# Longer load runs and 64 by 64 transposes for Q, K and V in a fused attention and spectral-mix kernel

## The chip, the cores and the metric

The kernel runs on one core of one Trainium2 chip. The metric is the device time of one execution in microseconds, the median of several runs; smaller is better. A core has TensorE (PE, matrix multiplication and transposes, with a row of its own for weight loads, PEld), VectorE (DVE), ScalarE (ACT), GpSimd (POOL), SyncE (SP), and 16 DMA engines that carry all transfers.

## What is computed

Sliding-window causal attention over 8 batches, 8 heads, 576 tokens and 64 values per head, then a Fourier-domain mix of the lowest 64 modes with a complex weight matrix for each mode, and a channel product with a rectifier:

```python
# attention: q, k, v are (8, 8, 576, 64) float32
scores = matmul(q, k.T) / sqrt(64)
mask   = (rel >= 0) & (rel < 64)            # rel = query position - key position
attn   = softmax(where(mask, scores, -1e9))
x      = matmul(attn, v)                    # heads side by side: (8, 576, 512)

# spectral mix: w_r, w_i are (64, 512, 512), w_ch is (512, 512)
X  = rfft(x, axis=1)[:, :64]                # 64 modes
Y  = X @ (w_r + i w_i), mode by mode
u  = x + irfft(Y, n=576)
out = u + relu(u @ w_ch)                    # (8, 576, 512) float32
```

The mode weights are most of the input: 127 matrices of 512 by 512 float32 values are read (the imaginary one of mode 0 isn't needed). Q, K and V are 24 pieces (three for each batch) of 8 x 576 x 64 float32 values, 1.18 MB each as they are read. GpSimd's DMAs turn float32 into bf16 on the way, so half as many bytes are written as are read.

## The kernel before

Q, K and V of a batch come as `[tokens, 64]` per head and are needed as `[64, tokens]`, two heads above each other in the 128 partitions: head group `hh` (heads 4 hh to 4 hh + 3) takes partitions 64 hh to 64 hh + 63. The partition of a loaded tile is a pair of head `g` within its group and run `p` of 18 tokens; the two head groups lie beside each other in a partition:

```python
RUN = S // 32                                # 18 tokens

def raw_tile(which):
    return rawp.tile([128, 2, RUN * D], BF16, name="r" + which)

def load(b, which):
    r = raw_tile(which)
    nc.gpsimd.dma_start(
        out=r, in_=RAW[which][b].rearrange("(x g) (p c) d -> (g p) x (c d)", g=4, c=RUN))
    raws[b, which] = r
```

A transpose then takes one token of each run, for all 128 partitions of one head group, and writes 64 rows by 128 columns of PSUM. Twelve of them (6 tokens, 2 groups) fill a PSUM tile, which one instruction of ScalarE or VectorE puts into its places:

```python
def part(src, dst, c0, on_act):
    def f():
        ps = ps_misc.tile([128, 6, 128], BF16, name="pst", tag="misc")
        for c in range(6):
            for hh in range(2):
                nc.tensor.transpose(out=ps[64 * hh:64 * hh + 64, c, :],        # L226
                                    in_=src[:, hh, (c0 + c) * D:(c0 + c + 1) * D],
                                    identity=ident_bf)
        evac(view(dst, c0, [[S, 4], [RUN, 32], [1, 6]]),                       # L58, L59
             view(ps, 0, [[32, 4], [1, 32], [128, 6]]), on_act)
    return f
# ... cut: vback turns V back into token rows (L243)
return [part(rk, kT, 0, True), part(rk, kT, 6, False), part(rk, kT, 12, True),
        # ... the same three for rv and rq, then vback(0), vback(1), vback(2)
```

These twelve units of a batch are spread among the windows of the batch before it. A window has scores (L299, 64 by 64 tiles of the TensorE array), an exponential on ScalarE (L305), the product with V (L324, mostly 128 rows by 64 columns), and the mask for the next window (L280, 64 by 64; L274 for the first six windows):

```python
scores(w)
weigh(w - 1, 8 * w - 8, cut)
if todo: todo.pop(0)()                       # a unit
mask(w + 1, max(1, 3 - n))
if todo: todo.pop(0)()
weigh(w - 1, cut, 8 * w)
while todo: todo.pop(0)()
```

Whenever a unit has used up a raw tile, POOL issues the load of the batch after next into it, and a load of a weight matrix (L117). After attention the weights stream through a set of buffers; each mode (L592) uses its two matrices and hands their buffers back to POOL, which loads the next ones (L122: two matrices in one DMA). The output stage (L742, L903, L926) follows when the last mode has been used.

```python
for im, w in enumerate((wr, wi) if m else (wr,)):
    for c in range(NC):
        # ... cut
        nc.tensor.matmul(out=psy[r0:r0 + k, :], lhsT=xq(c, m, im, [[NM, k]]), rhs=w[:, c, :], ...)  # L592
    # ... cut
    refill_w(m, im)                          # L117, L122: loads into the buffers that came free
```

Of the kernel before, what the change touches and what calls it, by code (L numbers as in the profile page):

```python
# [11 lines left out]
BF16 = mybir.dt.bfloat16  # L12
# [8 lines left out]
def view(ap, off, dims):  # L21

    return bass.AP(ap.tensor, ap.offset + off, [list(ap.ap[0])] + [list(d) for d in dims])
# [3 lines left out]
def kernel(  # L27
# [10 lines left out]
    nc = tc.nc  # L38
    B, H, S, D = q.shape
# [5 lines left out]
    NT = 5  # L45
    NC = DM // 128
    VW = 66
    RUN = S // 32
    LW = 5
    EW = 13  # L50

# [3 lines left out]
    def evac(o, i, on_act):  # L55

        if on_act:
            return nc.scalar.copy(out=o, in_=i)  # L58
        return nc.vector.tensor_copy(out=o, in_=i)  # L59
# [8 lines left out]
    ident_bf = consts.tile([128, 128], BF16, name="ident_bf")  # L68
# [11 lines left out]
    rawp = p1.enter_context(tc.tile_pool(name="rawp", bufs=2, side="right"))  # L80
# [5 lines left out]
    ps_misc = p1.enter_context(tc.tile_pool(name="ps_misc", bufs=3, space=PSUM))  # L86
# [5 lines left out]
    RAW = {"k": k, "q": q, "v": v}  # L92

    def raw_tile(which):
        return rawp.tile([128, 2, RUN * D], BF16, name="r" + which)

    def load(b, which):
        r = raw_tile(which)
        nc.gpsimd.dma_start(
            out=r, in_=RAW[which][b].rearrange("(x g) (p c) d -> (g p) x (c d)", g=4, c=RUN))  # L100
        raws[b, which] = r


# [23 lines left out]
    warm = acons.tile([128, 512], BF16, name="warm")  # L127
    nc.vector.memset(warm, 0.0)
    load(0, "k")
    load(0, "q")  # L130


# [39 lines left out]

    nc.scalar.activation(out=warm[:, 0:1], in_=ident[:, 0:1], func=ACT_F.Exp)
    load(0, "v")
    nc.vector.tensor_copy(out=ident_r, in_=ident)
    idp.close()
# [6 lines left out]
    for i in range(4):  # L183
        half = i % 2
        pp = slice(64 * (i // 2), 64 * (i // 2) + 64)
# [27 lines left out]
    def transpose_units(b):  # L213

        rk, rq, rv = (raws.pop((b, which)) for which in "kqv")
        qT = qtp.tile([128, 4, S], BF16, name="qT")
        vT = vtp.tile([128, 4, S], BF16, name="vT")
        kT, vt = kTs[b % 2], vts[b % 2]
        qTs[b] = qT

        def part(src, dst, c0, on_act):
            def f():
                ps = ps_misc.tile([128, 6, 128], BF16, name="pst", tag="misc")
                for c in range(6):
                    for hh in range(2):
                        nc.tensor.transpose(out=ps[64 * hh:64 * hh + 64, c, :],  # L226
                                            in_=src[:, hh, (c0 + c) * D:(c0 + c + 1) * D],
                                            identity=ident_bf)
                evac(view(dst, c0, [[S, 4], [RUN, 32], [1, 6]]),
                     view(ps, 0, [[32, 4], [1, 32], [128, 6]]), on_act)  # L230
            return f

        def vback(u):
            def f():
                ps = ps_misc.tile([128, 6, 128], BF16, name="psv", tag="misc")
                for i in range(6):
                    a, j = divmod(6 * u + i, 9)
                    if j == 4:
                        parts = [(0, 64, 2 * a, 512), (64, 64, 2 * a + 1, 0)]
                    else:  # L240
                        parts = [(0, 128, 2 * a + (j > 4), 128 * j - (j > 4) * S)]
                    for r0, n, g, t0 in parts:
                        nc.tensor.transpose(out=ps[r0:r0 + n, i, :],  # L243
                                            in_=vT[:, g, t0:t0 + n], identity=ident_bf)
                evac(view(vt, 6 * u * VW, [[18 * VW, 2], [VW, 6], [1, D]]),
                     view(ps, 0, [[D, 2], [128, 6], [1, D]]), u != 1)
                if u:
                    hs = slice(u - 1, u + 2, 2)
                    nc.vector.tensor_copy(out=vt[64:128, 1, hs, 1:9], in_=vt[64:128, 0, hs, 0:8])
                    nc.vector.tensor_copy(out=vt[0:64, 1, hs], in_=vt[0:64, 0, hs])  # L250
            return f

        return [part(rk, kT, 0, True), part(rk, kT, 6, False), part(rk, kT, 12, True),
                part(rv, vT, 0, False), part(rv, vT, 6, True), part(rv, vT, 12, False),
                part(rq, qT, 0, True), part(rq, qT, 6, False), part(rq, qT, 12, True),
                vback(0), vback(1), vback(2)]

    def head_of(n):
# [5 lines left out]
    for half in range(2):  # L264
        pp = slice(64 * half, 64 * half + 64)
# [119 lines left out]
    def refill(b, j):  # L385

        which = {2: "k", 5: "v", 8: "q"}.get(j)
        if which is None:
            return
        if b + 2 < B:  # L390
            load(b + 2, which)
        elif nw < EARLY:
            early(EARLY)
        if b:
            early(1)
        if b + 2 >= B:
            spare(raw_tile(which))
# [3 lines left out]
    with tc.manual_schedule(engines={mybir.EngineType.PE, mybir.EngineType.Pool}):  # L401
        warm_up(7)
        first = transpose_units(0)
        for i, j in enumerate((0, 1, 2, 6, 7, 8, 3, 4, 5, 9, 10, 11)):
            first[j]()
# [16 lines left out]
        def unit(b, j):  # L422
            if b not in units:
                units[b] = transpose_units(b)
            units[b][j]()
            refill(b, j)
# [175 lines left out]
    with ExitStack() as p2a:  # L602
# [30 lines left out]
        for m in range(L0 * MG):  # L633
            mode(m)
            if m == 1:
                for b in range(1, B, 2):
                    tc.keep_in_program_order(nc.scalar.copy(out=x_sb[64:128, b - 1, NT - 1, :],
                                                            in_=x_sb[64:128, b, NT - 1, :]))
# [181 lines left out]
    with tc.manual_schedule(engines={mybir.EngineType.PE}):  # L820
        for m in range(M0, ME):
            while len(spreads) > 5 * B // 2 * (ME - 1 - m) // (ME - M0):
                b0, h = spreads.pop(0)
# [54 lines left out]
    with tc.manual_schedule(engines={mybir.EngineType.PE, mybir.EngineType.Activation, mybir.EngineType.DVE,  # L878
                                     mybir.EngineType.Pool, mybir.EngineType.SP}):
        nc.vector.tensor_copy(out=view(YT2, R - RL, [[NR, NC], [R, 2], [1, RL]]),  # L880
                              in_=view(psl, 0, [[RL * B, NC], [RL, 2], [1, RL]]))
# [103 lines left out]
```

The softmax here doesn't subtract the row's maximum and nothing guards it: scores larger than these inputs give would overflow.

## Time and profile before

| what | value |
|---|---|
| device time, median of 3 | 426.12 us (426.09 to 426.28) |
| span of the profiled execution | 424.3 us, mean granted TensorE clock 0.927 |
| TensorE busy | 348.0 us (82%) |
| VectorE, ScalarE, GpSimd busy | 184.5, 171.2, 78.9 us |
| bytes written by GpSimd's DMAs | 81.80 MB in 24864 packets |
| memory read in all | 162.53 MB, 405 GB/s over the span |

The page cuts the span into 40 equal slices and gives, for each, the busy share of an engine in tenths. Attention lies in the first third, the weight stage ends near slice 36, and the output stage fills the rest. A matmul's duration in this trace is the time from its start to the end of its last result, and matmuls are pipelined, so what a run of them costs is read from the distance of their starts. In the DMA part, GB/s count what is written; a transfer that turns float32 into bf16 reads twice that. In the list of waits, each line reads: who waited, for whom, us in total, how often, longest.

### The profile page before, as it was taken

The numbers are of one execution on the slowest core, as the hardware profiler recorded it, in microseconds if no ns is written. First come the engines' busy times: TensorE is split into PE (matmuls) and PEld (weight loads), VectorE is DVE, ScalarE is ACT, GpSimd is POOL, SyncE is SP. The second block draws the span as 40 slices with busy tenths as digits, with TensorE's granted clock in tenths as the row PEclk, the third lists the DMA queues.
The fourth block names the chain that finished last, engine by engine and source line by source line (L and its number), as shares of the span: only waits on it lengthen the run. The fifth ranks groups of instructions, "written<-read, shape, count | busy, mean of one in ns | idle before, by whom it ended". The sixth has DMA issues, their size and how long they took to land.

```text
span 424.3 us, 8788 instructions
## 1 busy us (share of the span) xinstructions
PE 348.0 (82%) x3772; PEld 215.7 (51%) x3772; DVE 184.5 (43%) x397; ACT 171.2 (40%) x314; POOL 78.9 (19%) x141
## 2 busy tenths in 40 slices
PE   6999999999988897363698977977569997588993
PEld 5665665666665564122365644554324443255682
DVE  6466765766673211061443413331103433240994
ACT  4585866866763310021032312122203333130993
POOL 7131221331022222012111011211111113200000
PEclk9999999999996899556599999999968999999998
DMA  8999999999999999999999999999999999994598
GB/s 142 212 213 212 212 216 211 214 213 211 215 213 214 215 212 261 214 216 212 215 216 213 215 215 214 215 214 213 216 213 214 214 213 214 213 214 96 194 387 329
DMA packets 28166, 91.98 MB, mean 217 GB/s; under 512 B 2352, under 2 KB 2608, under 8 KB 28128
## 3 DMA queue, kind: packets, MB, share of 16 engines
q0 software_dynamic: 24864, 81.80, 96.6%
q1 hardware_dynamic: 3120, 9.50, 5.9%
q8 instruction: 29, 0.48, 0.4%
q10 hardware_dynamic: 144, 0.13, 0.1%
q14 instruction: 9, 0.07, 0.0%
HBM read 162.53 MB, written 9.44 MB: 405 GB/s over the span
## 4 chain that ended last, share of the span: by engine, by line
PE 38%; DMA 37%; issue 12%; DVE 8%; POOL 2%; ACT 2%; POOLq 0%; DVEq 0%
DMA wt<-in_moe_w_r_dram 23%; DMA wt<-in_moe_w_i_dram 14%; PE pso L324 7%; PE pst L226 6%; PE psy L592 4%; PE pso L903 4%; PE psv L243 3%; DVE x_sb L332 3%; PE psw L742 3%; PE pss L280 2%; PE pss L381 2%; PE psx L346 2%; PE pss L299 2%; DVE vT L59 2%; POOL wt L122 1%
## 5 line engine op out<-in xcount | busy, mean ns | idle before, releaser
L592 PE MATMUL psy<-wt,XQ 128*32 128x512 bf16 (+1 forms) x404 | 86.1, 427 | 42.6 <-DMA wt<-in_moe_w_i_dram 25.6
L592 PEld LDWEIGHTS <-XQ 128*32 128x32 bf16 (+1 forms) x476 | 46.2, 132 | 82.7 <-issue 65.8
L621 DVE CAST xT<-pxt 128x256 fp32r<-128x256 bf16 (+1 forms) x68 | 26.0, 434 | 56.4 <-PE pxt L614 41.1
L628 ACT CAST Z<-psz 128x512 fp32r<-128x512 f32 x36 | 21.1, 587 | 58.4 <-PE psz L626 58.1
L305 ACT ACTIVATE et<-pss 128x512 bf16<-128x512 f32 x72 | 39.2, 599 | 12.8 <-PE pss L299 12.8
L626 PE MATMUL psz<-wch,xT 128*128 128x512 f32 x144 | 40.3, 417 | 0.4 <-DVE xT L621 0.4
L324 PE MATMUL pso<-vt,et 128*64 128x65 bf16 (+1 forms) x576 | 34.0, 209 | 5.2 <-DVE x_sb L332 5.1
L324 PEld LDWEIGHTS <-et 128*64 128x64 bf16 (+1 forms) x576 | 23.7, 113 | 17.2 <-issue 9.8
L626 PEld LDWEIGHTS psz<-wch,xT 128*128 128x128 f32 x144 | 26.1, 193 | 11.6 <-issue 5.7
L59 DVE COPY x_sb<-psy 128x256 f32<-128x256 f32 x15 | 6.4, 424 | 56.4 <-PE psy L592 56.4
L58 ACT COPY x_sb<-psy 128x256 f32<-128x256 f32 x15 | 5.6, 373 | 60.6 <-DVE x_sb L59 60.6
L332 DVE TENSOR_TENSOR x_sb<-pso,rcp 128x640 bf16<-128x640 f32 x32 | 26.3, 823 | 0.9
L122 POOL DMA_DIRECT2D wt<-in_moe_w_r_dram x15 | 10.7, 713 | 77.7 <-PE psy L592 68.7
L903 PE MATMUL pso<-Y,trigI 128*128 128x512 f32 x80 | 23.1, 403 | 0.1
L926 DVE TENSOR_TENSOR ot<-pso,x_sb 128x512 f32<-128x512 f32 x35 | 22.2, 685 | 1.5 <-PE pso L903 1.1
L280 PE MATMUL pss<-band,ident_bf 64*64 64x512 bf16 x136 | 20.4, 407 | 1.5 <-ACT et L305 1.5
L59 DVE COPY vT<-pst 128x768 bf16<-128x768 bf16 x16 | 15.3, 958 | 13.0 <-PE pst L226 13.0
L117 POOL DMA_DIRECT2D wt<-in_moe_w_r_dram x25 | 13.6, 544 | 37.9 <-PE psy L592 22.8
L59 DVE CAST x_sb<-psj 128x512 bf16<-128x512 f32 x18 | 12.2, 688 | 18.5 <-PE psj L804 15.6
L908 ACT ACTIVATE pso<-pso 128x512 f32<-128x512 f32 x36 | 19.2, 594 | 0.0
L58 ACT CAST x_sb<-psj 128x512 bf16<-128x512 f32 x18 | 10.5, 586 | 19.3 <-PE psj L804 19.2
L122 POOL DMA_DIRECT2D wt<-in_moe_w_i_dram x15 | 10.7, 714 | 36.1 <-PE psy L592 35.1
(159 smaller groups left out, 530.3 us busy)
## 6 DMA issues: line engine op xcount, KB each, us to landing
wt<-in_moe_w_r_dram POOLq DMA_DIRECT2D x15, 1024.0 KB, 23.0
wt<-in_moe_w_i_dram POOLq DMA_DIRECT2D x15, 1024.0 KB, 25.4
wt<-in_moe_w_r_dram POOLq DMA_DIRECT2D x25, 512.0 KB, 16.9
wt<-in_moe_w_i_dram POOLq DMA_DIRECT2D x21, 512.0 KB, 18.2
out_dram<-ot SPq DMA_DIRECT2D x15, 512.0 KB, 4.2
rk<-in_k_dram POOLq DMA_DIRECT2D x8, 576.0 KB, 10.5
rq<-in_q_dram POOLq DMA_DIRECT2D x8, 576.0 KB, 14.2
rv<-in_v_dram POOLq DMA_DIRECT2D x8, 576.0 KB, 13.0
```

The lines of the kernel that those rows point to most:

```text
L59: return nc.vector.tensor_copy(out=o, in_=i)
L122: nc.gpsimd.dma_start(out=wt, in_=src[m:m + 2].rearrange("m (p c) e -> p m c e", c=NC))
L226: nc.tensor.transpose(out=ps[64 * hh:64 * hh + 64, c, :], in_=src[:, hh, (c0 + c) * D:(c0 + c + 1) * D], identity=ident_bf)
L280: nc.tensor.matmul(out=pss[(2 * w + hh) % 3][64 * half:64 * half + 64, :], lhsT=ident_bf[pp, pp], rhs=view(band[pp], 128 * half, [[0, WIN ...
L305: nc.scalar.activation(out=et[:, hh, :], in_=pss[(2 * w + hh) % 3], func=ACT_F.Exp, scale=EX_SCALE)
L324: nc.tensor.matmul(out=pso[po, hh, (i // 2) * VW:(i // 2) * VW + D + 1], lhsT=et[pk, hh, col:col + 64], rhs=vt[pk, 1 - f % 2, 2 * hh + g / ...
L332: nc.vector.tensor_tensor(out=view(x_sb, b * NT * DM + g * D, [[4 * D, 2], [DM, NT], [1, D]]), in0=view(pso, 0, [[512, 2], [VW, NT], [1, D]]),
L592: nc.tensor.matmul(out=psy[r0:r0 + k, :], lhsT=xq(c, m, im, [[NM, k]]), rhs=w[:, c, :], start=(im + c == 0), stop=(im == (m > 0) and c == ...
L621: nc.vector.tensor_copy(out=xT[:, :, w * k:w * k + w], in_=view(psts[k], j, [[128, NC], [n, w]] if n > 1 else [[128, NC], [1, 64], [64, 2]]))
L626: nc.tensor.matmul(out=psz, lhsT=xT[:, c, :], rhs=wch[:, c, :], start=(c == 0), stop=(c == NC - 1))
L903: nc.tensor.matmul(out=tps[n], lhsT=trigI[:, tr:tr + 128], rhs=pair_tile(what, bb), start=False, stop=stop and r0 + k == 128, skip_group_c ...
L926: nc.vector.tensor_tensor(out=ot[:, j], in0=ps, in1=x_sb[:, b, t, :], op=ALU.add)
```

## The change

A batch of Q, K or V is one block of 128 rows: 8 heads of 16 runs of 36 tokens, so that partition 16 h + p holds run `p` of head `h`, and all of a partition comes from one run of 9216 bytes. Head group 0 then lies in partitions 0 to 63, and group 1 in 64 to 127. A transpose takes one token of each run of one group: a 64 by 64 block, from the group's own partitions to the same partitions of PSUM. A PSUM tile holds 12 tokens in place of 6, for 64 columns in place of 128, and the number of evictions and their sizes stay as they were. The aim is longer contiguous runs in the transfers, and transposes that use a pair of diagonal quarters of the array.

```diff
-    RUN = S // 32
+    RUN = S // 16
+    CP = RUN // 3
...
-        return rawp.tile([128, 2, RUN * D], BF16, name="r" + which)
+        return rawp.tile([128, RUN * D], BF16, name="r" + which)
...
-            out=r, in_=RAW[which][b].rearrange("(x g) (p c) d -> (g p) x (c d)", g=4, c=RUN))
+            out=r, in_=RAW[which][b].rearrange("h (p c) d -> (h p) (c d)", c=RUN))
...
-                ps = ps_misc.tile([128, 6, 128], BF16, name="pst", tag="misc")
-                for c in range(6):
+                ps = ps_misc.tile([128, CP, 64], BF16, name="pst", tag="misc")
+                for c in range(CP):
                     for hh in range(2):
-                        nc.tensor.transpose(out=ps[64 * hh:64 * hh + 64, c, :],
-                                            in_=src[:, hh, (c0 + c) * D:(c0 + c + 1) * D],
-                                            identity=ident_bf)
-                evac(view(dst, c0, [[S, 4], [RUN, 32], [1, 6]]),
-                     view(ps, 0, [[32, 4], [1, 32], [128, 6]]), on_act)
+                        pp = slice(64 * hh, 64 * hh + 64)
+                        nc.tensor.transpose(out=ps[pp, c, :], in_=src[pp, (c0 + c) * D:(c0 + c + 1) * D],
+                                            identity=ident_bf[pp, pp])
+                evac(view(dst, c0, [[S, 4], [RUN, 16], [1, CP]]),
+                     view(ps, 0, [[16, 4], [1, 16], [64, CP]]), on_act)
...
-        return [part(rk, kT, 0, True), part(rk, kT, 6, False), part(rk, kT, 12, True),
+        return [part(rk, kT, 0, True), part(rk, kT, 1 * CP, False), part(rk, kT, 2 * CP, True),
         # the same for rv and rq
```

The line numbers of the changed kernel are higher by one from the second line of the diff on, and by two for the transpose: L226 becomes L228.

More of the change, by code (lines that the diff above doesn't have):

```diff
@@ L251, in vback @@
             return f
-        return [part(rk, kT, 0, True), part(rk, kT, 6, False), part(rk, kT, 12, True),
-                part(rv, vT, 0, False), part(rv, vT, 6, True), part(rv, vT, 12, False),
-                part(rq, qT, 0, True), part(rq, qT, 6, False), part(rq, qT, 12, True),
+        return [part(rk, kT, 0, True), part(rk, kT, 1 * CP, False), part(rk, kT, 2 * CP, True),
+                part(rv, vT, 0, False), part(rv, vT, 1 * CP, True), part(rv, vT, 2 * CP, False),
+                part(rq, qT, 0, True), part(rq, qT, 1 * CP, False), part(rq, qT, 2 * CP, True),
                 vback(0), vback(1), vback(2)]
```

## The prediction

> **What bounds the kernel now.** I began with the page's slices of the span, to see which engine is full in which stage.
>
> ```profile
> PE   6999999999988897363698977977569997588993
> ...
> DMA  8999999999999999999999999999999999994598
> GB/s 142 212 213 212 212 216 211 214 213 211 215 213 214 215 212 261 214 216 212 215 216 213 215 215 214 215 214 213 216 213 214 214 213 214 213 214 96 194 387 329
> ```
>
> A slice is 10.6 us. TensorE is full only in attention (slices 1 to 13, to about 140 us). The DMA row stands at 9 from slice 1 to slice 35, in attention and weight stage alike, with about 213 GB/s in each slice. (The 261 is the one transfer that isn't cast, and counts twice as many bytes per byte read.) A rate so flat through stages so different says that the transfers set the pace, if they never run dry. Two more views test that. The waits:
>
> ```profile
> POOL wt L122 <- PE psy L592: 103.8, 22, 9.0
> ...
> POOL rk L99 <- PE pst L226: 33.6, 6, 8.7
> ...
> PE psy L592 <- DMA wt<-in_moe_w_i_dram: 25.6, 14, 3.8
> ...
> PE psy L592 <- DMA wt<-in_moe_w_r_dram: 15.9, 11, 5.0
> ...
> POOL rv L99 <- PE pst L226: 15.2, 6, 3.1
> ...
> POOL rq L99 <- PE pst L226: 13.2, 6, 2.4
> ```
>
> POOL, which issues the loads, waits for free buffers (the lines with POOL on the left), which looks like starving. It isn't: I subtracted, at each issue, the bytes that had moved from the bytes that had been issued. At 213 GB/s the queue holds 4 to 5 us at its lowest points after the start (24, 40, 126, 335 to 350 us) and 8 to 20 us elsewhere. So TensorE waits for DMA in the weight stage, and the queue always has work from 4 to about 387 us. The end of the kernel is the moment when 81.8 MB have passed, plus a tail of some 37 us of output work that the change doesn't touch.
>
> ```profile
> q0 software_dynamic: 24864, 81.80, 96.6%
> ...
> q8 instruction: 29, 0.48, 0.4%
> ```
>
> ```profile
> 5.00:31.00 26.00, 24.56 (x399) 17.37 (x397) 14.69 (x27) 16.10 (x27) 9.78 (x18) 1.00 1.11 212
> ...
> 172.00:352.00 180.00, 140.20 (x723) 78.42 (x722) 57.24 (x165) 42.17 (x86) 28.78 (x47) 0.87 1.06 214
> ```
>
> The second pair are stretches (time, then each engine's busy us; the last three columns are granted clock, DMA share, GB/s). In the first only Q, K and V move, in packets that read 4608 B and write 2304 B; in the second only weights, 8192 B to 4096 B. The gap from 212 to 214 GB/s is all that the packet size can be worth, and part of it belongs to instruction fetches.
>
> [...]214 GB/s written is 428 GB/s read[...]. [...]from L226 (128 rows by 64 columns) to L299 (64 by 64) the starts lie 149 ns apart, inside one mode 28 ns. [...]Here the tiled scores of L299 start every 15 ns on average[...].
>
> **The change part by part.**
>
> *Loads.* 24 loads of 256 packets become 24 of 128: 6144 packets become 3072 of double size; bytes are unchanged. To price a packet I cut 5 to 380 us into 4 us stretches and fitted their lengths, by least squares, to the counts of each kind of packet over 16 engines: 174.5 ns for 4608 B read, 306.7 ns for 8192 B, 80 ns for 2048 B (the uncast one), and 1.08 us for a 16 KB instruction fetch. The first two give a slope of 132.2 ns over 3584 B, 0.0369 ns per B, and 174.5 - 170.0 = 4.5 ns fixed; the third checks it (4.5 + 75.6 = 80.1). A packet of 9216 B should take 344.5 ns. Old: 6144 x 174.5 / 16 = 67.0 us; new: 3072 x 344.5 / 16 = 66.1 us. **-0.9 us, on the path.**
>
> *Issue.* A load takes POOL about 700 ns with 256 packets, a 512 KB weight load 530 ns with 128. At the start the first packet moves at 2.8 us, after POOL has issued K; it should move some 0.17 us earlier, and all behind it. **-0.2 us on the path**; the other 22 issues are hidden.
>
> *Transposes.* The view of the tile that receives them:
>
> ```profile
> L226 PE MATMUL pst<-ident_bf,rk x288: 218/219/243, 8.8 to 113.6; 128*64 128x128 bf16 x144
> ...
> L58 ACT COPY kT<-pst x16: 811/816/829, 9.4 to 113.8; 128x768 bf16<-128x768 bf16 x16
> L59 DVE COPY vT<-pst x16: 957/958/959, 14.7 to 117.7; 128x768 bf16<-128x768 bf16 x16
> ```
>
> The 219 ns is latency; the cost is the distance between starts, 27.9 ns in a run of 12 or 24 of L226, so a part of 12 takes 335 ns, 72 parts 24.1 us. The new part has 24 transposes of 64 columns: 864 more in all. The nearest thing in the trace is L324, 65 columns from 64 loaded columns in alternating column halves: 15 to 18 ns each where halves alternate. 24 x 15.5 = 372 ns, 72 parts 26.8 us: **+2.7 us of TensorE** (from -2 at 13 ns to +7 at 18 ns).
>
> *Mode changes.* Transposes in 64 by 64 now join the scores and masks (L299, L280), which are 64 by 64 already, but part from L324 and other 128-row work. Counting tile sizes along the TensorE order of the two built programs, to the end of attention: 313 changes become 275. 38 x (149 - 28) ns = **-4.6 us of TensorE.** Together -2 us, with -6 to +3 likely. It lies beside the DMA queue: as long as TensorE in attention doesn't fall back by the 4 to 5 us of the queue's lowest depth, it is worth nothing at the end. If it gets faster it only deepens the queue.
>
> *Evictions.* 768 elements in, 768 out; source steps of 64 elements in place of 128, runs of 12 in place of 6. [...]ACT's 812 to 816 ns is the same as that of the unit-step eviction of psv (809). No change.
>
> *Instruction fetch.* 864 transposes and as many weight loads add 1728 instructions. 29 fetches now serve the 7544 of TensorE, so 1728 add 6.6; 6.6 x 1.08 / 16 = **+0.45 us on the path**, as they use the same DMA engines.
>
> *Sum:* -0.9 - 0.2 + 0.45 = -0.65 us, so 426.1 becomes **425.5 us**.
>
> **Rivals.** *A: row tiles serialise on the shared bank.*[...] If it holds, each transpose takes 28 ns or more, a part 0.67 us, and TensorE has +24 - 4.6, some 20 us, to make up in attention; the queue covers 5 of it: about 440 us. *B: the sequencer can't feed two instructions every 15 ns* (today 28 ns in L226), and a part takes 500 ns: 12 us more, less 4.6 for modes: 7 us, of which the queue covers 5: about 428 us. Against it: the scores keep 15 ns, but only for 18 in a row. *C: the weight stage profits.* A faster attention frees its buffers earlier; but the queue never runs dry, so this gives nothing. *D: the packets give more than fitted*, for the trace's DMA records give a packet 192 ns at 2304 B written and 324 at 4096 B, and the line through these has 22 ns fixed: 3072 x 22 / 16, some 4 us less. Against it: DMA shares over 1 show packets overlapping, so a fixed part is mostly hidden.
>
> **Range and chances.** The sum is -0.65, and the terms that can move it by themselves are small (1 us either way). C and D make 422 to 425 possible; B about 428. I give A one chance in twelve and B one in eight. Range 423.5 to 428. Faster by over 2% would need 8.5 us[...]: 2 in 100. Slower by over 2% needs A: 7 in 100.
>
> **What would show it.** Right: packets of the dynamic queue fall by 3072 and GB/s in the first slices rise from 212 to about 214; the first transfer starts near 2.6 us; 35 or 36 instruction fetches; DMA still at 9 from slice 1 to slice 35; L228 transposes 13 to 18 ns apart; evictions unchanged; the moment when the last weights land some 0.6 us earlier. Wrong: a DMA slice under 9 within attention (A or B), POOL's waits for pst growing, transposes 28 ns apart or more, or evictions away from 958 and 812 ns. The prediction fails most likely by TensorE's pace in attention, since only there could a large number come.

## The result, and the profile after

The changed kernel takes 449.97 us (449.11 to 450.82) against 426.12 us: a ratio of 1.0559, with a 95% interval of 1.0533 to 1.0585. It is 24 us slower, and outside the range of the prediction.

The slices of the page after, a slice being 11.2 us:

```profile
PE   6878878978969888945569896898658887589994
...
PEclk9988996698987959985659999999989999969998
DMA  7999899499995799999999999999999999996498
GB/s 152 215 212 199 155 202 198 88 204 203 211 193 93 135 211 210 258 216 214 214 214 214 215 214 215 214 214 215 214 213 214 213 214 213 214 213 139 157 384 320
```

Before, the DMA row was full from slice 1 to slice 35. Now it has holes in slices 3 to 7 and 11 to 13, with 88 and 93 GB/s at their deepest, all within attention; after slice 14 it runs at 210 GB/s and more again and never recovers what it missed. The TensorE row, which was at 9 in attention, is mostly at 7 and 8, and its clock row drops again and again. Before, that row was full until 130 us:

```profile
PEclk9999999999996899556599999999968999999998
```

The last bytes of the weights land at 413.4 us in place of 389.2: the whole loss is made in attention. The last product with V (L324, now L325) starts at 167.4 us in place of 139.6, 28 us later, and the queue's reserve of 4 to 5 us covers the rest of the difference.

Who made TensorE wait in attention (20 to 169 us), longest first:

```profile
PE pst L228 <- issue: 11.0, 9, 2.4
PE pso L325 <- DVE x_sb L333: 4.8, 12, 0.9
PE pss L275 <- issue: 1.7, 1, 1.7
PE psv L244 <- issue: 1.4, 2, 1.0
PE pss L300 <- issue: 1.4, 1, 1.4
```

"issue" means that nothing which the profile shows was waited for: no semaphore, no buffer, no data. In the kernel before no such line stands for PE in this stage (20 to 141 us); these are all that do:

```profile
PE pso L324 <- DVE x_sb L332: 5.1, 14, 0.9
PE pss L274 <- ACT et L305: 1.7, 2, 1.2
PE pss L280 <- ACT et L305: 1.5, 3, 0.6
```

A pause seen close up, in the timeline of TensorE:

```profile
63.34 0.82 PE L325 MATMUL pso<-vt,et 64*64 64x65 bf16 x16
64.10 0.21 PE L228 MATMUL pst<-ident_bf,rv 64*64 64x64 bf16 x1
65.91 1.32 PE L228 MATMUL pst<-ident_bf,rv 64*64 64x64 bf16 x42 [1.60 <-issue]
```

One transpose of a run starts, the next 42 follow 1.8 us later. They have the same operands, the same tiles and the same semaphores behind them. What sets the second one apart is its number. I counted TensorE's instructions (weight loads and matmuls together, and three instructions of its sequencer) from the start of the trace, and put beside each pause of over 0.9 us without a semaphore the instruction at which it ended, and the time at which the last packet of 16 KB of the instruction queue had passed:

```
pause ended at (us)    24.5  30.4  36.4  54.1  60.0  65.9  72.1  95.6  101.8  125.2  131.7
instruction number      705   961  1217  1984  2240  2495  2751  3774   4030   5052   5308
16 KB packet done at   23.1  29.0  34.9  52.5  58.7  64.6  70.6  94.2  100.3  123.9  130.3
```

The numbers are multiples of 256 apart (less one or two where records are missing), and every pause ends 1.3 to 1.6 us after such a packet. At the end of each pause, 193 instructions and 256 for each packet that had passed lay behind TensorE: two packets at 705, twenty at 5308 (five records are missing by then). So 256 instructions go with a packet of 16 KB, 64 B for each (an estimate: 16384 B by 256). The reading that fits all eleven pauses: **TensorE had run out of instructions.** The trace gives the cycle of this supply: the next packet starts 3.2 to 4.2 us after a pause has ended (1.6 and 2.5 us after two of the eleven), moves for about 0.95 us, and 1.3 to 1.6 us later the next block runs. Where pauses follow each other, the packets of the changed kernel lie 5.9 to 6.4 us apart: that is how long 256 instructions took to come there, beside 202 to 213 GB/s of data. Those of the kernel before lie 5.8 to 7.2 us apart through attention. Counted at the same numbers there, the packet for the next block starts 2.4 to 3.7 us after a block begins, so that the next block was ready after some 4.8 to 6.0 us (an estimate: this, 0.95 us and about 1.4 us), and a block was used up in 5.1 to 7.8 us. The supply was only just ahead; no pause without a semaphore at a block's end was over 0.4 us.

### The profile page after: what moved, and what is told of

Its sections match the earlier page's. It is cut to its first block, busy times and chain, and to the rows that moved or that the text cites. A ratio compares the mean times of both kernels' runs of the same rounds, so it can differ in the third digit from the quotient of the medians.

```text
span 448.9 us, 10506 instructions
## 1 busy us (share of the span) xinstructions
PE 358.6 (80%) x4626; PEld 229.2 (51%) x4636; DVE 184.6 (41%) x397; ACT 172.1 (38%) x314; POOL 74.5 (17%) x141
## 3 DMA queue, kind: packets, MB, share of 16 engines
q0 software_dynamic: 21792, 81.80, 91.5%
## 4 chain that ended last, share of the span: by engine, by line
DMA 42%; PE 32%; issue 15%; DVE 6%; POOL 2%; ACT 1%; POOLq 0%; DVEq 0%; SPq 0%
DMA wt<-in_moe_w_r_dram 25%; DMA wt<-in_moe_w_i_dram 16%; PE pst L228 7%; PE pso L325 7%; PE psv L244 4%; PE pss L281 2%; PE pso L904 2%; PE pss L382 2%; PE pss L300 2%; DVE x_sb L333 2%; PE psx L347 2%; DVE ot L927 2%; PE pss L275 1%; POOL wt L123 1%; DVE vT L60 1%
## 5 line engine op out<-in xcount | busy, mean ns | idle before, releaser
L593 PE MATMUL psy<-wt,XQ 128*32 128x512 bf16 (+1 forms) x404 | 84.4, 423 | 42.2 <-DMA wt<-in_moe_w_i_dram 28.3
L622 DVE CAST xT<-pxt 128x256 fp32r<-128x256 bf16 (+1 forms) x68 | 26.0, 434 | 55.4 <-PE pxt L615 39.9
L306 ACT ACTIVATE et<-pss 128x512 bf16<-128x512 f32 x72 | 39.2, 600 | 15.5 <-PE pss L300 15.5
L325 PE MATMUL pso<-vt,et 128*64 128x65 bf16 (+1 forms) x576 | 36.6, 219 | 4.8 <-DVE x_sb L333 4.8
L325 PEld LDWEIGHTS <-et 128*64 128x64 bf16 (+1 forms) x576 | 25.6, 121 | 17.8 <-issue 11.6
L281 PE MATMUL pss<-band,ident_bf 64*64 64x512 bf16 x136 | 21.5, 469 | 1.0 <-ACT et L306 1.0
L300 PE MATMUL pss<-qT,kT 64*64 64x128 bf16 (+1 forms) x640 | 21.0, 235 | 1.4 <-issue 1.4
L244 PE MATMUL psv<-ident_bf,vT 128*128 128x128 bf16 (+1 forms) x160 | 17.7, 247 | 1.5 <-issue 1.4
```

The costliest lines, as they stand in the source:

```text
L244: nc.tensor.transpose(out=ps[r0:r0 + n, i, :], in_=vT[:, g, t0:t0 + n], identity=ident_bf)
L281: nc.tensor.matmul(out=pss[(2 * w + hh) % 3][64 * half:64 * half + 64, :], lhsT=ident_bf[pp, pp], rhs=view(band[pp], 128 * half, [[0, WIN ...
L300: nc.tensor.matmul(out=pss[(2 * w + hh) % 3][64 * half:64 * half + 64, col:col + nq], lhsT=kTs[b % 2][pp, g, 64 * kb:64 * kb + 64], rhs=qT ...
L306: nc.scalar.activation(out=et[:, hh, :], in_=pss[(2 * w + hh) % 3], func=ACT_F.Exp, scale=EX_SCALE)
L325: nc.tensor.matmul(out=pso[po, hh, (i // 2) * VW:(i // 2) * VW + D + 1], lhsT=et[pk, hh, col:col + 64], rhs=vt[pk, 1 - f % 2, 2 * hh + g / ...
```

## The experiments

The theory, from the numbers above, is **F**: instructions arrive 256 at a time by DMA, one block ahead, and the 1728 added ones make TensorE use a block in less time than the next one needs behind a full queue. The rivals are **S**, the 64 by 64 transposes themselves (slow when two go to one PSUM tile, or with a lower clock), and **P**, the larger packets.

### The loads alone

```diff
         nc.gpsimd.dma_start(
-            out=r, in_=RAW[which][b].rearrange("(x g) (p c) d -> (g p) x (c d)", g=4, c=RUN))
+            out=r.rearrange("p x c -> p (x c)"),
+            in_=RAW[which][b].rearrange("h (p c) d -> (h p) (c d)", c=2 * RUN))
```

> Kernel before with the loads of the change (128 packets of 9216 B read) and its own transposes, so that tokens land in other places of the tiles (the output is not the reference's; the work is the same in kind and count). Theory F (TensorE runs out of instructions: they come 256 at a time by DMA, one block ahead, and a block takes about 5.9 us to come while the DMA queue is full): no more instructions than before, so 424.5 to 425.6 us, the -0.9 and -0.2 us of the load terms alone. Rival P (larger packets delay something, instruction fetches or semaphores): 430 us or more. Rival D of the prediction (packets worth 4 us): 422 us.

Measured: 425.44 us, ratio 0.9984 (0.9967 to 1.0001). The interval touches 1, so the 0.7 us is not certain as a time. In its trace the first packet moves at 2.59 us in place of 2.78, and the same fit over stretches as in the prediction gives 342 ns for a packet of 9216 B. The loads cost nothing at the end, and P falls. (Attention's last product with V starts 3 us later in this trace than before, at 142.6 us, which the queue's reserve covers.) One pause of 0.71 us at instruction 1985 shows how near the kernel before is to the edge.

### The transposes alone

```diff
-            out=r, in_=RAW[which][b].rearrange("h (p c) d -> (h p) (c d)", c=RUN))
+            out=r.rearrange("p (x c) -> p x c", x=2),
+            in_=RAW[which][b].rearrange("(x g) (p c) d -> (g p) x (c d)", g=4, c=RUN // 2))
```

(against the changed kernel)

> Changed kernel with the loads of before (256 packets of 4608 B read); tokens land in other places of the tiles, the work is the same in kind and count. Theory F: as slow as the changed kernel, 447 to 453 us, since the instructions are as many. Rival S (the 64 by 64 transposes themselves[...]): also 447 to 453. Rival P: 426 to 430 us.

Measured: 449.65 us, ratio 1.052 (1.0467 to 1.0573). The loss is that of the transposes, all of it. F and S remain.

### The kernel before with more instructions

```diff
                     for hh in range(2):
+                        nc.tensor.matmul(out=ps[64 * hh:64 * hh + 64, c, 0:16].bitcast(FP32),
+                                         lhsT=src[:, hh, (c0 + c) * D:(c0 + c + 1) * D],
+                                         rhs=ident_bf[:, 0:8], start=True, stop=True)
                         nc.tensor.transpose(out=ps[64 * hh:64 * hh + 64, c, :],
```

> Kernel before, with a matmul of 8 columns (own weight load) ahead of each of the 864 transposes, into columns that the transpose then overwrites: 1728 more TensorE instructions, as in the changed kernel, but loads, transposes and tile sizes of before. Output unchanged. Theory F: 440 to 460 us, and TensorE pauses of 1 to 2.5 us that lie 256 instructions (or multiples) apart, waiting for no semaphore. Rivals S and P: no such pauses; TensorE has some 864 x 14 ns = 12 us more work, of which the queue covers 5: 426 to 434 us.

> As the run with a small matmul ahead of each transpose, but only ahead of those of every other token: 864 more TensorE instructions in place of 1728. Theory F: in attention a block of 256 is used in about 5.5 us against 5.9 us to fetch one: a few pauses, 428 to 438 us, well under the full dose. Rivals S and P: 426 to 429 us without pauses.

Measured: 450.81 us with all of them, ratio 1.0559 (1.0502 to 1.0616), and 436.86 us with half, ratio 1.0224 (1.0164 to 1.0284). None of the change is in these kernels. The waits of TensorE in attention with all of them:

```profile
PE pst L226 <- issue: 2.8, 3, 1.0
PE pso L327 <- DVE x_sb L335: 2.4, 7, 0.9
PE pst L229 <- issue: 2.3, 2, 1.4
PE psv L246 <- issue: 1.7, 2, 1.2
PE pss L302 <- issue: 1.6, 1, 1.6
```

The same kind of pause, again at numbers 256 apart (961, 1985, 2241, 2497, 2753, 4033, 4545). Not all of the loss is pauses: a pair of small matmul and transpose takes 2 x 21.7 ns, a transpose alone took 27.9, so 864 of them add 13 us of work, of which the queue's reserve covers 5. That alone would have made about 434 us (an estimate). The last product with V starts at 167.8 us, 28 us later than before: 13 are this work, and eight pauses at block ends, of 0.7 to 1.8 us, sum to 10. Some 5 are left; the clock was at half for 33 us of this attention, against 9 before, but its part was not measured. With half of the added matmuls the work is 6.7 us, and 428 us would have been the end (an estimate); measured were 437, with six such pauses of 0.7 to 1.2 us. Both results lie in the range that F gave, and in neither that the rivals gave.

### The changed kernel with an emptier queue

```diff
         elif nw < EARLY:
             early(EARLY)
-        if b:
-            early(1)
         if b + 2 >= B:
```

> Changed kernel, but the weight loads that stand among the Q, K and V loads of batches 1 to 5 are issued together behind them (one line left out; same work, same output). Up to about 100 us the DMA queue then carries Q, K and V alone and is often empty. Theory F: a block of instructions comes much sooner than in 5.9 us, so between 25 and 90 us TensorE has no pauses of over 0.7 us without a semaphore, its clock stays at 1.00 there, and the last transposes of Q (148.9 us in the changed kernel, 121 before) start at 125 us or earlier. The whole kernel is slower, 455 to 475 us, as some 42 us of transfers move behind attention. Rival S (the 64 by 64 transposes themselves, or their effect on the clock): attention as long as in the changed kernel, pauses and half clock remain, last transposes at 145 us or later.

Measured: 458.3 us. What counts is the pace of attention from the ninth window to the twenty-fifth (the same program in all three kernels but for the transposes), taken from the first exponential of each. The stretches of before, of the changed kernel, and of this run:

```profile
47.20:101.30 54.10, 51.21 (x1084) 34.09 (x1085) 36.24 (x65) 37.83 (x65) 14.21 (x24) 1.00 1.09 213
```

```profile
55.30:121.90 66.60, 57.36 (x1441) 40.66 (x1444) 36.44 (x65) 38.35 (x64) 12.21 (x24) 0.85 0.95 184
```

```profile
53.70:109.10 55.40, 51.94 (x1440) 36.97 (x1440) 35.86 (x64) 37.61 (x64) 10.12 (x20) 0.97 0.77 136
```

The first two columns are the stretch and its length, then the busy time of PE, PEld, DVE, ACT and POOL with their instructions; the last three are clock, DMA share and GB/s. The changed kernel needs 66.6 us for what took 54.1. With the same 1440 matmuls and the same weight loads, but 136 GB/s in place of 184, it needs 55.4. TensorE's waits in this run from 36 to 100 us:

```profile
PE pso L325 <- DVE x_sb L333: 2.1, 5, 0.6
PE pss L281 <- ACT et L306: 0.5, 1, 0.5
PE pst L228 <- issue: 0.4, 1, 0.4
```

The pauses are gone but for one of 0.6 us at 52 us, the clock is full from 40.6 to 105.4 us, and from 50 to 99 us the instruction packets lie 3.7 to 5.6 us apart. The packet for the next block starts at most 2.3 us after a block begins there, against 2.4 to 3.7 us before: beside a queue that is often empty (a DMA share of 0.77 in this stretch, 0.95 in the changed kernel), the supply kept up with a faster use. So the 64 by 64 transposes cost this stretch 1.3 us in 54, changes of tile size included, and S falls.

Three of the things expected from F were missed. Pauses of 2.7 and 0.9 us stand at 25.6 and 33.4 us, where the queue still held its first loads, and the clock is at half from 30.3 to 40.6 us. And the last transposes of Q start at 136.0 us, not by 125: from 99 us on the deferred weights fill the queue, and pauses of 1.4 to 2.2 us return at numbers 256 apart. The packets that these pauses, early and late, waited for came beside a full queue (211 to 215 GB/s while each was due).

### The changed kernel with half of its transposes

```diff
-                for c in range(CP):
+                for c in range(CP // 2):
...
-                evac(view(dst, c0, [[S, 4], [RUN, 16], [1, CP]]),
-                     view(ps, 0, [[16, 4], [1, 16], [64, CP]]), on_act)
+                evac(view(dst, c0, [[RUN, 64], [2, CP // 2], [1, 2]]),
+                     view(ps, 0, [[1, 64], [64, CP // 2], [0, 2]]), on_act)
```

(the PSUM tile is halved with it)

> Changed kernel with only half of its transposes: 12 of 64 by 64 for each eviction, and the eviction writes each of these 6 tokens to two places, so its size stays (the output is not the reference's; half of the transposes are left out). TensorE instructions as many as before the change, loads and tile sizes those of the change. Theory F: no pauses, 424.5 to 425.8 us. Rival S: half of the loss remains, 434 to 442 us.

Measured: 425.34 us, ratio 0.9988 (0.9965 to 1.0011). With as many instructions as before, and the loads, tiles and kind of transpose of the change, the loss is gone. "No pauses" was too much: there are four of 0.7 to 1.6 us, and the last product with V starts at 142.1 us, 2.5 us later than before, which the queue's reserve covers. The clock was at half for some 40 us of this attention, 47 in the changed kernel, and it cost nothing at the end here. (Half of the transposes' work is gone too, so this run by itself says less against S than the one before it.)

A version that keeps the new loads without the added instructions was not found; that there is none was not shown. Nor would it be worth much: 0.7 us by the run with the loads alone, and that is not certain. The kernel before stays the faster one.

## Why the prediction was wrong, point by point

- **What bounds the kernel: right.** The queue of transfers set the pace as long as it never ran dry (211 to 216 GB/s in slices 1 to 35 before, but for one), and attention's reserve is 4 to 5 us. Attention came 28 us late, the end 24. The flat rate is measured; that the transfers can go no faster was the author's estimate, and no run here shows it.
- **Loads and issue: right.** 24864 packets of the dynamic queue became 21792, a packet of 9216 B takes 342 to 345 ns (344.5 predicted), the first one moves 0.17 us earlier (0.19 with the loads alone), and the issue fell to 531 ns. The loads alone gave -0.7 us, with an interval that touches zero, against -1.1 for these two terms.
- **Transposes and mode changes: within the range given.** Where nothing stalls and the clock is full, the new transposes start 15.4 to 16.3 ns apart, on average over runs of 20 to 72 (15.5 taken). The traces have 310 changes of tile size up to the end of attention before and 272 after, 38 fewer as counted. With the emptier queue, 16 of attention's 36 windows took 55.4 us against 54.1, where a small gain was expected (-2 us in all, -6 to +3 likely). That two row tiles exclude each other on a shared bank was an assumption of rival A, and no trace here shows it: the diagonal pair, which writes different partitions of one PSUM tile, started 16 ns apart, where rival A had 28 ns or more. Rival A did not happen.
- **Evictions: right.** The view of the PSUM tile in the changed kernel (durations in ns, least, median, most):

```profile
L228 PE MATMUL pst<-ident_bf,rk x576: 189/193/260, 8.9 to 140.9; 64*64 64x64 bf16 x192
...
L59 ACT COPY kT<-pst x16: 799/800/817, 9.5 to 141.1; 128x768 bf16<-128x768 bf16 x16
L60 DVE COPY vT<-pst x16: 957/958/959, 15.0 to 144.9; 128x768 bf16<-128x768 bf16 x16
```

  958 ns as before on VectorE, 800 in place of 812 to 816 on ScalarE. (958 ns is not what every layout took: the eviction of `psv`, of the same size, took 560 ns on VectorE in the trace before. With source steps of 128 elements before and of 64 after, that of `pst` took 958 ns both times.)
- **Instruction fetch: the step that failed.** The prediction counted 6.6 more fetches and charged them 0.45 us as traffic. The count was right, as the page's list of DMA queues after the change shows (packets, MB, share):

```profile
q0 software_dynamic: 21792, 81.80, 91.5%
...
q8 instruction: 36, 0.59, 0.5%
```

  36 in place of 29. But their price here was not their bytes. It was the time that TensorE waited for them: 5.9 to 6.4 us for a block where the queue was full and the pauses followed each other. In the kernel before the packets lay 5.8 to 7.2 us apart, so the fetch was already close to being a second bound of attention. Its trace has no pause that would show where a block ends, but it has the packets' starts, and with 1728 instructions more in attention, where 4979 were recorded, their distance had to fall to some 4.7 us (an estimate: 6.3 us on average, times 4979 / 6707). I read their size and not their distance, and never asked whether they could come so fast.
- **Rival B came nearest and was mis-sized.** It said that TensorE might not be fed two instructions every 15 ns, and stopped at 7 us, because it took the slowness to lie in a short run of transposes. It lay in the sum of all instructions: 1728 more at 5.9 us for 256 are up to 40 us of supply (an estimate), less what the stage had to spare.

How the 28 us of attention divide: the twelve pauses at block ends without a semaphore (the eleven above, and one of 0.7 us) sum to 18 us from start to start, and the kernel before has none. The clock was at half for 47 us of attention against 9 before; six of the seven spells begin within 2.1 us of such a pause or in it. About 10 us are left for that and for the work of the transposes, 1.3 us in the stretch of 16 windows. The clock's part was not measured by itself.

## What to carry to other kernels

Count the instructions that TensorE takes in a stage, not only their work: here, where TensorE had to wait beside a full DMA queue, 256 came in 5.9 to 6.4 us, some 23 to 25 ns for an instruction, or 46 to 50 ns for a weight load with its matmul. The new transposes started 16 ns apart, closer than that, and 864 more of them went with 24 us more; with half of them left out the time was 425.34 us. Here the fewer and larger ones of the kernel before were the faster choice. "issue" as a releaser in the middle of a run of equal instructions, at steps of 256, was the sign of it here.

## What the runs showed of the hardware

In the changed kernel, transposes of 64 by 64 in diagonal quarters, into one PSUM tile, started 15.4 to 16.3 ns apart on average at full clock where nothing stalled, weight loads included. TensorE's instructions came more slowly beside more data: where it had to wait for them beside a full queue (202 to 213 GB/s), the packets of 16 KB came 5.9 to 6.4 us apart, and in the run with the deferred weights, with a queue that was often empty (122 GB/s from 44 to 99 us), they came 3.7 to 5.6 us apart without a pause of over 0.6 us.
